# Chunks 1 to 3 of x by DMA transpose, and chunk 0's first layer with k as the outer loop, in a fused two-layer kernel

## The chip, the cores and the metric

One core of one Trainium2 chip. The metric is the device time of one execution in microseconds (us). "Span" is the time from the first to the last instruction in a profile; it is about 1.8 us shorter than the device time of the same run. A run is called slow when it is over 1.5% above the fastest run of its kernel.

Engines in the profile: PE is TensorE (PEld its weight loads), ACT is ScalarE, DVE is VectorE, POOL is GpSimd, SP issues DMA. A final q, as in SPq, means the engine's sequencer.

## The reference

```python
# x [1, 2048, 640], w1 [640, 1536], b1 [1536], w2 [1536, 640], b2 [640], all bfloat16
h = einsum("bsd,df->bsf", x, w1) + b1
h = relu(h) ** 2
out = einsum("bsf,fd->bsd", h, w2) + b2
```

## The kernel before

It works on four chunks of 512 rows of x. The contraction over D = 640 has five steps of 128, called k. F = 1536 gives twelve groups of 128, called j. For each chunk, PE makes twelve first-layer groups of five 128x512 matmuls, ACT adds b1 and applies relu, DVE squares, and PE then makes eight second-layer groups of twelve matmuls, 128x320 each (the very last group is cut in two). The first-layer matmuls of this kernel read x with D on the partitions (`rhs=xT[:, k, ...]`), so x is transposed. Here PE does that through PSUM, against an identity matrix, and DVE copies the result out. The transposes of chunk c+1 stand between the first-layer groups of chunk c.

```python
# loads on SP, in this order: x tiles 0-1, x tiles 2-3, then
sp.dma_start(out=w1_sb[:, :, 0:W1A], in_=w1_v[:, :, 0:W1A]).then_inc(s_w1a, 16)   # W1A = 384
sp.dma_start(out=w1_sb[:, :, W1A:F], in_=w1_v[:, :, W1A:F]).then_inc(s_w1b, 16)
# x chunk 1, b2, w2; POOL loads x chunks 2 and 3 after w2
# ... (cut)
def t_group(t):                    # one 128x640 tile of x: five PE transposes
    # ... waits (cut)
    for k in range(KD):
        ins = pe.transpose(out=t_ps[:, bank, k * P:(k + 1) * P],
                           in_=x_sb[:, t, k * P:(k + 1) * P], identity=ident[:])
def mm1_group(c, j):               # k is the inner loop
    # ... waits on s_w1a, s_w1b, s_xT (cut)
    for k in range(KD):
        ins = pe.matmul(h_ps[:, bank, :], lhsT=w1_sb[:, k, j * P:(j + 1) * P],
                        rhs=xT[:, k, c * CH:(c + 1) * CH],
                        start=(k == 0), stop=(k == KD - 1))
# ... (cut)
dummy(NDUM0)                       # 4 matmuls on zeros
# transpose of b1 (cut)
for t in range(TPC):
    t_group(t)                     # chunk 0
dummy(NDUM1)                       # 1 matmul on zeros
for c in range(NCH):
    for j in range(KF):
        mm1_group(c, j)
        if c + 1 < NCH and j in TPOS:          # TPOS = [6, 7, 8, 9]
            t_group((c + 1) * TPC + TPOS.index(j))
    # second layer of chunk c (cut)
# DVE: four copies of chunk 0's xT, then dve.wait_ge(s_b2, 16), then all squares
```

Of the kernel before, what the change touches and what calls it, by code (L numbers as in the profile page):

```python
# [5 lines left out]
ACT = mybir.ActivationFunctionType  # L6
ALU = mybir.AluOpType
BF16 = mybir.dt.bfloat16
FP32 = mybir.dt.float32


def bass_standalone__dense_activation_squared_relu__prompt_kernel(
# [8 lines left out]
    P = 128  # L21
# [10 lines left out]
    NH = 3  # L32
    NO = 3
    NT = 2
    NR = 4

    W1A = 384
    NDUM0 = 4
    NDUM1 = 1
    LAST_SPLIT = [(0, 320), (320, 160), (480, 160)]  # L40

    TPOS = [6, 7, 8, 9]

    x_v = x[0].rearrange("(i p) d -> p i d", p=P)
# [6 lines left out]
    with ExitStack() as es:  # L51
# [9 lines left out]
        x_sb = sb("x_sb", [P, NST, D], BF16)  # L61
# [12 lines left out]
        h_ps = ps("h_ps", [P, NH, 512], FP32)  # L74
        o_ps = ps("o_ps", [P, NO, 512], FP32)
        t_ps = ps("t_ps", [P, NT, 1024], BF16)
# [5 lines left out]
        s_xc1 = sem("s_xc1")  # L82
        s_xc2 = sem("s_xc2")
        s_xc3 = sem("s_xc3")
        s_w1a = sem("s_w1a")
        s_w1b = sem("s_w1b")
        s_w2 = sem("s_w2")
        s_b1 = sem("s_b1")
        s_b2 = sem("s_b2")
        s_b1ps = sem("s_b1ps")  # L90
# [11 lines left out]
        s_x0t = [s_xa, s_xa, s_xb, s_xb]  # L102
        s_xc = [None, s_xc1, s_xc2, s_xc3]
# [9 lines left out]
        NG = len(groups)  # L113
        out_dmas = []
# [6 lines left out]
        @block.sync  # L121
        def _(sp):
            sp.dma_start(out=x_sb[:, 0:2, :], in_=x_v[:, 0:2, :]).then_inc(s_xa, 16)  # L123
            sp.dma_start(out=x_sb[:, 2:4, :], in_=x_v[:, 2:4, :]).then_inc(s_xb, 16)  # L124
            sp.dma_start(out=w1_sb[:, :, 0:W1A], in_=w1_v[:, :, 0:W1A]).then_inc(s_w1a, 16)
            sp.dma_start(out=w1_sb[:, :, W1A:F], in_=w1_v[:, :, W1A:F]).then_inc(s_w1b, 16)
            sp.dma_start(out=x_sb[:, TPC:2 * TPC, :], in_=x_v[:, TPC:2 * TPC, :]).then_inc(s_xc1, 16)
            sp.dma_start(out=b2_bc[:], in_=b2_v).then_inc(s_b2, 16)
            sp.dma_start(out=w2_sb[:], in_=w2_v).then_inc(s_w2, 16)
            for (cnt, i, c0, nc_) in out_dmas:  # L130
                sp.wait_ge(s_osb, cnt)
                sp.dma_start(out=out_v[:, i, c0:c0 + nc_], in_=o_sb[:, i, c0:c0 + nc_]).then_inc(s_out, 16)
            sp.wait_ge(s_out, 16 * len(out_dmas))

        @block.gpsimd
        def _(pool):
            pool.memset(ident[:], 0.0).then_inc(s_ms, 1)  # L137
            pool.affine_select(  # L138
                out=ident[:],
                in_=ident[:],  # L140
                compare_op=ALU.not_equal,
                fill=1.0,
                base=0,
                pattern=[[-1, P]],
                channel_multiplier=1,
            ).wait_op(s_ms, 1, "sem-ge").then_inc(s_id, 1)
            pool.wait_ge(s_w2, 16)
            pool.dma_start(out=x_sb[:, 2 * TPC:3 * TPC, :], in_=x_v[:, 2 * TPC:3 * TPC, :]).then_inc(s_xc2, 16)  # L148
            pool.dma_start(out=x_sb[:, 3 * TPC:4 * TPC, :], in_=x_v[:, 3 * TPC:4 * TPC, :]).then_inc(s_xc3, 16)  # L149

        @block.tensor
        def _(pe):
            o_ps_bf = o_ps[:].bitcast(BF16)

            def dummy(nd):
                for _ in range(nd):
                    pe.matmul(o_ps[:, 0, :], lhsT=zeros[:, 0:P], rhs=zeros[:, :], start=True, stop=True)  # L157

            def t_group(t):
                c, i = divmod(t, TPC)  # L160
                bank = t % NT
                if c == 0:
                    if i % 2 == 0:
                        pe.wait_ge(s_x0t[i], 16)
                elif i == 0:
                    pe.wait_ge(s_xc[c], 16)
                for k in range(KD):
                    ins = pe.transpose(  # L168
                        out=t_ps[:, bank, k * P:(k + 1) * P],
                        in_=x_sb[:, t, k * P:(k + 1) * P],  # L170
                        identity=ident[:],
                    )
                    if k == 0 and t >= NT:
                        ins.wait_op(s_xT, t - NT + 1, "sem-ge")
                    if k == KD - 1:
                        ins.then_inc(s_T, 1)

            def mm1_group(c, j):
                n = c * KF + j
                bank = n % NH  # L180
                if c == 0 and j == 0:
                    pe.wait_ge(s_w1a, 16)
                if c == 0 and j * P == W1A:
                    pe.wait_ge(s_w1b, 16)
                if j == 0:
                    pe.wait_ge(s_xT, TPC * (c + 1))
                for k in range(KD):
                    ins = pe.matmul(  # L188
                        h_ps[:, bank, :],
                        lhsT=w1_sb[:, k, j * P:(j + 1) * P],  # L190
                        rhs=xT[:, k, c * CH:(c + 1) * CH],
                        start=(k == 0),
                        stop=(k == KD - 1),
                    )
                    if k == 0 and n >= NH:
                        ins.wait_op(s_r, n - NH + 1, "sem-ge")
                    if k == KD - 1:
                        ins.then_inc(s_h, 1)

            def mm2_group(m):  # L200
                i, c0, nc_ = groups[m]
                bank = m % NO
                c = i // TPC
                first_of_chunk = (i % TPC == 0) and c0 == 0
                if m == 0:
                    pe.wait_ge(s_w2, 16)
                if m == NO - 1:
                    pe.wait_ge(s_b1T, 1)
                if m >= NO and first_of_chunk:
                    pe.wait_ge(s_osb, m - NO + 1)  # L210
                for j in range(KF):
                    ins = pe.matmul(  # L212
                        o_ps[:, bank, 0:nc_],
# [4 lines left out]
                    )  # L218
                    if first_of_chunk:
                        ins.wait_op(s_r2, c * KF + j + 1, "sem-ge")  # L220
                    elif j == 0 and m >= NO:
                        ins.wait_op(s_osb, m - NO + 1, "sem-ge")
                    if j == KF - 1:
                        ins.then_inc(s_o, 1)

            pe.wait_ge(s_z, 1)
            dummy(NDUM0)
            pe.wait_ge(s_id, 1)
            pe.wait_ge(s_b1, 16)
            pe.transpose(  # L230
                out=o_ps_bf[:, NO - 1, 0:KF],
                in_=b1_row[:, :],
                identity=ident[0:KF, 0:KF],
            ).then_inc(s_b1ps, 1)
            for t in range(TPC):
                t_group(t)
            dummy(NDUM1)

            m = 0
            for c in range(NCH):  # L240
                for j in range(KF):
                    mm1_group(c, j)
                    if c + 1 < NCH and j in TPOS:
                        t_group((c + 1) * TPC + TPOS.index(j))
# [5 lines left out]
        def _(act):  # L250
            o_ps_bf = o_ps[:].bitcast(BF16)
            act.dma_start(out=b1_row[:], in_=b1_v).then_inc(s_b1, 16)
            act.activation(out=junk[:, 0:1], in_=zeros[:, 0:1], func=ACT.Relu).wait_op(s_z, 1, "sem-ge")  # L253
            act.activation(out=b1T[:], in_=o_ps_bf[:, NO - 1, 0:KF], func=ACT.Identity).wait_op(  # L254
                s_b1ps, 1, "sem-ge"
            ).then_inc(s_b1T, 1)
            act.wait_ge(s_b1T, 1)
            for n in range(NCH * KF):
                c, j = divmod(n, KF)
                if n >= NR:  # L260
                    act.wait_ge(s_r2, n - NR + 1)
                act.activation(  # L262
                    out=r_sb[:, n % NR, :],
                    in_=h_ps[:, n % NH, :],
# [3 lines left out]
                ).wait_op(s_h, n + 1, "sem-ge").then_inc(s_r, 1)  # L268

        @block.vector  # L270
        def _(dve):
            def t_evac(t):
                bank = t % NT
                dve.tensor_copy(  # L274
                    out=xT[:, :, t * P:(t + 1) * P],
                    in_=t_ps[:, bank, 0:KD * P].rearrange("p (k s) -> p k s", k=KD),
                ).wait_op(s_T, t + 1, "sem-ge").then_inc(s_xT, 1)

            def square(c, j):
                n = c * KF + j  # L280
                dve.tensor_tensor(  # L281
# [4 lines left out]
                ).wait_op(s_r, n + 1, "sem-ge").then_inc(s_r2, 1)  # L286

            def o_evac(m):
                i, c0, nc_ = groups[m]
                dve.tensor_tensor(  # L290
                    out=o_sb[:, i, c0:c0 + nc_],
                    in0=o_ps[:, m % NO, 0:nc_],
                    in1=b2_bc[:, c0:c0 + nc_],
                    op=ALU.add,
                ).wait_op(s_o, m + 1, "sem-ge").then_inc(s_osb, 1)

            dve.memset(zeros[:], 0.0).then_inc(s_z, 1)  # L297
            for t in range(TPC):
                t_evac(t)
            dve.wait_ge(s_b2, 16)  # L300
            m = 0
            for c in range(NCH):
                for j in range(KF):
                    if c + 1 < NCH and j in TPOS:
                        t_evac((c + 1) * TPC + TPOS.index(j))
                    square(c, j)
# [31 lines left out]
```

## Time and profile before

| | before |
|---|---|
| device time, median of the first 4 runs | 120.69 us (120.03 to 122.18) |
| span of the first profile (a slow run, 122.18 us) | 120.4 us |
| PE busy | 114.2 us, 95% of the span |
| first matmul on w1 | 8.50 us |

The first view is the chain that ended last, in order of time, merged: start, duration, what ran. It is followed back from the last instruction to whatever released each step.

```profile
1.74 6.71 DMA w_sb<-in_w_dram
8.45 0.05 issue
8.50 7.24 PE h_ps L188 x23
...
18.33 0.28 PE t_ps L168 x5
18.61 1.08 PE h_ps L188 x5
...
24.84 13.04 PE o_ps L212 x96
...
51.95 13.04 PE o_ps L212 x96
...
92.15 10.74 PE h_ps L188 x49
...
105.05 13.08 PE o_ps L212 x108
```

From 8.50 us, when the first part of w1 has landed, to the end, the chain lies on PE. Steady rates can be read from it: 0.216 us per first-layer matmul (1.08 for five), 0.136 per second-layer matmul (13.04 for 96), and 0.28 us for five transposes. The line of 7.24 us for 23 matmuls does not fit the first rate: 0.31 us each.

The timeline of this kernel from 6 to 12.8 us shows why (start, duration, engine, line, operation; in brackets the idle time before it):

```profile
6.30 0.63 PE L157 MATMUL o_ps<-zeros 128*128 128x512 bf16 x1
8.49 0.13 PEld L188 LDWEIGHTS h_ps<-xT,w_sb 128*128 128x128 bf16 x2 [2.15 <-DMA w_sb<-in_w_dram]
8.50 4.65 PE L188 MATMUL h_ps<-xT,w_sb 128*128 128x512 bf16 x11 [1.56 <-DMA w_sb<-in_w_dram]
8.90 0.15 PEld L188 LDWEIGHTS h_ps<-xT,w_sb 128*128 128x128 bf16 x1 [0.28 <-issue]
9.33 0.15 PEld L188 LDWEIGHTS h_ps<-xT,w_sb 128*128 128x128 bf16 x1 [0.28 <-issue]
...
12.31 0.15 PEld L188 LDWEIGHTS h_ps<-xT,w_sb 128*128 128x128 bf16 x1 [0.28 <-issue]
```

Weight loads start 0.43 us apart and take 0.15 us where later ones take 0.10. PE runs at half its later rate for the first ten matmuls or so, which costs about 2.1 us (10 x 0.21). What ends the stretch, and what sets its length, this trace does not show. The profile prints a granted clock of 1.00 for the whole run, but that says nothing here: the trace holds no clock record before 12.80 us, which is just where the slow stretch ends, and time without a record is printed as 1.00. So it is the spacing of the instructions that shows the slow stretch.

### The profile page before, as it was taken

Reading aid. Unit: us, or ns where it says so; the run is one execution under the profiler, and the core shown is the slowest. Engines: PE = TensorE matmul, PEld = TensorE weight load, DVE = VectorE, ACT = ScalarE, POOL = GpSimd, SP = SyncE. Lnnn points to the kernel's source line nnn. Section 1 sums busy time; section 2 is a strip of 40 time slices with the busy share of each in tenths; the row PEclk is TensorE's granted clock in tenths of the full one; section 3 lists DMA queues with packets and bytes.
Section 4 is the critical chain, followed back from the end, with each engine's and each line's share of the span. In section 5 each row is a group of like instructions: output and inputs, shape, how many; then the busy total and the mean of one; then the engine's idle time right before and its main releaser. Section 6 shows DMA issues by size and latency. Waiting matters only on the chain.

```text
span 120.4 us, 1706 instructions
## 1 busy us (share of the span) xinstructions
PE 114.2 (95%) x714; PEld 67.9 (56%) x722; DVE 43.6 (36%) x98; ACT 34.7 (29%) x51; POOL 2.3 (2%) x8
## 2 busy tenths in 40 slices
PE   6749999999999999999999999999999999999992
PEld 1513445567776445567776445567776444477781
DVE  0330067542233337542233337542233334433331
ACT  4002464530000664530000664530000666610000
POOL 2000002300000000000000000000000000000000
PEclk9999999999999999999999999999999999999999
DMA  3999991671101100001101100001101100001112
GB/s 92 271 334 392 321 353 39 177 259 54 37 26 51 54 0 0 0 3 54 42 26 46 54 3 0 5 0 54 35 26 48 54 5 0 0 0 54 54 54 54
DMA packets 6991, 9.44 MB, mean 78 GB/s; under 512 B 712, under 2 KB 6088, under 8 KB 6984
## 3 DMA queue, kind: packets, MB, share of 16 engines
q1 hardware_dynamic: 6672, 8.03, 19.9%
q0 software_dynamic: 288, 1.31, 3.4%
q8 instruction: 5, 0.08, 0.3%
q14 instruction: 2, 0.02, 0.1%
q10 hardware_dynamic: 24, 0.00, 0.0%
HBM read 6.72 MB, written 2.62 MB: 78 GB/s over the span
## 4 chain that ended last, share of the span: by engine, by line
PE 91%; DMA 6%; SPq 1%; issue 1%; DVE 0%
PE h_ps L188 45%; PE o_ps L212 43%; DMA w_sb<-in_w_dram 6%; PE t_ps L168 3%; SPq L124 0%; SPq L123 0%; DVE o_sb L290 0%
## 5 line engine op out<-in xcount | busy, mean ns | idle before, releaser
L188 PE MATMUL h_ps<-xT,w_sb 128*128 128x512 bf16 x232 | 55.3, 390 | 2.0 <-DMA w_sb<-in_w_dram 1.6
L262 ACT ACTIVATE r_sb<-h_ps,b1T 128x512 bf16<-128x512 f32 x48 | 33.0, 687 | 69.2 <-PE h_ps L188 68.8
L212 PE MATMUL o_ps<-w_sb,r2T 128*128 128x320 bf16 (+1 forms) x396 | 52.8, 295 | 0.0
L212 PEld LDWEIGHTS o_ps<-w_sb,r2T 128*128 128x128 bf16 x396 | 38.1, 98 | 14.9
L188 PEld LDWEIGHTS h_ps<-xT,w_sb 128*128 128x128 bf16 x240 | 23.4, 100 | 28.5 <-issue 2.8
L281 DVE TENSOR_TENSOR r2T<-r_sb 128x512 bf16<-128x512 bf16 x48 | 20.2, 425 | 31.5 <-ACT r_sb L262 23.5
L290 DVE TENSOR_TENSOR o_sb<-o_ps,b_bc 128x320 bf16<-128x320 f32 (+1 forms) x33 | 15.9, 482 | 33.5 <-PE o_ps L212 33.5
L274 DVE COPY xT<-t_ps 128x640 bf16<-128x640 bf16 x16 | 7.9, 492 | 9.0 <-PE t_ps L168 8.9
L168 PEld LDWEIGHTS t_ps<-ident,x_sb 128*128 128x128 bf16 x80 | 6.2, 108 | 4.0 <-DMA x_sb<-in_x_dram 0.7
L168 PE MATMUL t_ps<-ident,x_sb 128*128 128x128 bf16 x80 | 7.8, 242 | 0.7 <-DMA x_sb<-in_x_dram 0.6
L157 PE MATMUL o_ps<-zeros 128*128 128x512 bf16 x5 | 2.5, 629 | 1.2 <-DVE zeros L297 1.2
L253 ACT ACT_TABLE_LOAD x1 | 1.3, 1283 | 1.4 <-PEq L323 1.4
L157 PEld LDWEIGHTS o_ps<-zeros 128*128 128x128 bf16 x5 | 0.6, 136 | 1.7 <-DVE zeros L297 1.2
L148 POOL DMA_DIRECT2D x_sb<-in_x_dram x1 | 0.9, 885 | 19.1 <-DMA w_sb<-in_w_dram 19.1
L149 POOL DMA_DIRECT2D x_sb<-in_x_dram x1 | 0.8, 751 | 0.0
L230 PEld LDWEIGHTS o_ps<-ident,b_row 12*128 12x128 bf16 x1 | 0.1, 98 | 1.0 <-issue 1.0
L297 DVE MEMSET zeros<- 128x256 uint32 x1 | 0.3, 272 | 0.9 <-PEq L323 0.9
L254 ACT ACTIVATE b1T<-o_ps 128x12 f32<-128x12 bf16 x1 | 0.2, 181 | 0.4 <-PE o_ps L230 0.4
L138 POOL TENSOR_SCALAR_AFFINE_SELECT ident<-ident 128x128 bf16<-128x128 bf16 x1 | 0.3, 289 | 0.1
L230 PE MATMUL o_ps<-ident,b_row 12*128 12x12 bf16 x1 | 0.2, 162 | 0.1
L137 POOL MEMSET ident<- 128x128 bf16 x1 | 0.2, 205 | 0.3 <-POOLq L323 0.3
L253 ACT ACTIVATE junk<-zeros 128x1 f32<-128x1 bf16 x1 | 0.2, 203 | 0.0
(4 smaller groups left out, 0.4 us busy)
## 6 DMA issues: line engine op xcount, KB each, us to landing
out_dram<-o_sb SPq DMA_DIRECT2D x15, 160.0 KB, 1.8
w_sb<-in_w_dram SPq DMA_DIRECT2D x1, 1920.0 KB, 15.2
w_sb<-in_w_dram SPq DMA_DIRECT2D x1, 1440.0 KB, 9.9
x_sb<-in_x_dram POOLq DMA_DIRECT2D x2, 640.0 KB, 5.3
x_sb<-in_x_dram SPq DMA_DIRECT2D x2, 320.0 KB, 3.3
x_sb<-in_x_dram SPq DMA_DIRECT2D x1, 640.0 KB, 11.0
w_sb<-in_w_dram SPq DMA_DIRECT2D x1, 480.0 KB, 6.7
b_bc<-in_b_dram SPq DMA_DIRECT2D x1, 160.0 KB, 11.1
```

The costliest lines, as they stand in the source:

```text
L148: pool.dma_start(out=x_sb[:, 2 * TPC:3 * TPC, :], in_=x_v[:, 2 * TPC:3 * TPC, :]).then_inc(s_xc2, 16)
L149: pool.dma_start(out=x_sb[:, 3 * TPC:4 * TPC, :], in_=x_v[:, 3 * TPC:4 * TPC, :]).then_inc(s_xc3, 16)
L157: pe.matmul(o_ps[:, 0, :], lhsT=zeros[:, 0:P], rhs=zeros[:, :], start=True, stop=True)
L168: ins = pe.transpose(out=t_ps[:, bank, k * P:(k + 1) * P], in_=x_sb[:, t, k * P:(k + 1) * P], identity=ident[:],)
L188: ins = pe.matmul(h_ps[:, bank, :], lhsT=w1_sb[:, k, j * P:(j + 1) * P], rhs=xT[:, k, c * CH:(c + 1) * CH], start=(k == 0), stop=(k == KD ...
L212: ins = pe.matmul(o_ps[:, bank, 0:nc_], lhsT=r2T[:, j, i * P:(i + 1) * P], rhs=w2_sb[:, j, c0:c0 + nc_], start=(j == 0), stop=(j == KF - 1),)
L230: pe.transpose(out=o_ps_bf[:, NO - 1, 0:KF], in_=b1_row[:, :], identity=ident[0:KF, 0:KF],).then_inc(s_b1ps, 1)
L253: act.activation(out=junk[:, 0:1], in_=zeros[:, 0:1], func=ACT.Relu).wait_op(s_z, 1, "sem-ge")
L262: act.activation(out=r_sb[:, n % NR, :], in_=h_ps[:, n % NH, :], func=ACT.Relu, bias=b1T[:, j:j + 1], scale=1.0,).wait_op(s_h, n + 1, "sem ...
L274: dve.tensor_copy(out=xT[:, :, t * P:(t + 1) * P], in_=t_ps[:, bank, 0:KD * P].rearrange("p (k s) -> p k s", k=KD),).wait_op(s_T, t + 1, " ...
L281: dve.tensor_tensor(out=r2T[:, j, c * CH:(c + 1) * CH], in0=r_sb[:, n % NR, :], in1=r_sb[:, n % NR, :], op=ALU.mult,).wait_op(s_r, n + 1, ...
L290: dve.tensor_tensor(out=o_sb[:, i, c0:c0 + nc_], in0=o_ps[:, m % NO, 0:nc_], in1=b2_bc[:, c0:c0 + nc_], op=ALU.add,).wait_op(s_o, m + 1, " ...
```

## The change

The intent is twofold. The PE transposes of chunks 1 to 3 are to leave the critical engine, with the transposing done by the DMA on the way in. And chunk 0 is to start as soon as one k slice of w1 has landed: with k outside, eight groups can each use slice 0 while slice 1 is under way. The eight groups of the pass hold a PSUM bank each, so the pass borrows the second layer's and the transposes' banks.

```diff
-            sp.dma_start(out=w1_sb[:, :, 0:W1A], in_=w1_v[:, :, 0:W1A]).then_inc(s_w1a, 16)
-            sp.dma_start(out=w1_sb[:, :, W1A:F], in_=w1_v[:, :, W1A:F]).then_inc(s_w1b, 16)
-            sp.dma_start(out=x_sb[:, TPC:2 * TPC, :], in_=x_v[:, TPC:2 * TPC, :]).then_inc(s_xc1, 16)
+            for k in range(KD):
+                sp.dma_start(out=w1_sb[:, k, :], in_=w1_v[:, k, :]).then_inc(s_w1k[k], 16)
 ... (b2, w2; then, after all loads have landed:)
+            for c in range(1, NCH + 1):
+                if c < NCH:
+                    sp.dma_start_transpose(
+                        out=xT[:, :, c * CH:(c + 1) * CH], in_=x2[c * CH:(c + 1) * CH, :]
+                    ).then_inc(s_xTc[c], 16)
+                    spw.wait_all([(s_xTc[c], 16)])
+                # ... the stores of chunk c-1, and a wait until they have landed (cut)
 ... (PE)
-            dummy(NDUM1)                # and NDUM0 = 4 becomes 5
+            for k in range(KD):
+                for j in range(NPASS):   # NPASS = 8
+                    # ... waits: slice k; xT of chunk 0 (cut)
+                    mm1_matmul(j, k, extra)
+            for j in range(NPASS, KF):
+                for k in range(KD):
+                    mm1_matmul(j, k, [(s_w1k[k], 16)])
 ... (later chunks: mm1 with k inside, waiting on s_xTc[c]; no t_group among them)
```

Four smaller things come along. A helper emits waits only where they are still needed. The wait of DVE on b2 moves from before the squares to the output additions. The last transposed tile of chunk 0 is copied out in two parts. And b1 is loaded through SP, before the w1 slices, and no longer through ACT.

## The prediction

Its fourth step is about the DMA transposes that bring in chunks 1 to 3, 640 KB each.

> **What bounds the kernel now.** TensorE, from 8.5 us on. In the chain of waits PE has 91% of the span: first-layer matmuls 45%, second-layer 43%, transposes 3%; before them stand 6.7 us of w1 load. Read in order of time, PE is released by the first w1 slice at 8.50 and then has no gap over 0.05 us until 118.1. Steady rates from the same view: 1.08 us per five 128x512 matmuls, 13.04 us per second-layer chunk of 96, 0.28 us per five transposes. The first ten or so matmuls start 0.43 us apart, later ones 0.216: about 2.1 us of slow start.
>
> **What changes.**
> 1. Sixty PE transposes (12 groups at 0.28 us) leave the critical chain: -3.3 us. Cross-check in the chain: the first layer takes 14.0 us in chunks 1 and 2 and 12.9 in chunk 3, which has no transposes among its matmuls.
> 2. PE starts earlier. It now waits for x and the 480 KB w1 slice, in 768-byte rows, landing at 8.45. After, the first slice is 384 KB in 3 KB rows. I expect the first real matmul near 7.2 us (6.8 to 8.0): -1.3 us. A later slice lands about each 1.1 us (384 KB at the roughly 370 GB/s of the load stage), while a pass of eight takes 3.4 us slow and 1.7 fast, so no pass waits.
> 3. New stall in chunk 0. K-outer over eight banks finishes no group until the fifth pass, so ACT begins all twelve activations (687 ns each) there. From the pass's start, ACT needs 0.4 + 12 x 0.70 = 8.8 us, the last square 0.48 more: 9.3. PE reaches the last matmul of the first output group after 1.73 + 4.3 + 1.5 = 7.5. Cost: +1.8 us, all critical.
> 4. [...] The first is issued when all loads have landed (about 18 us, earlier than w2's 20 now as one x load is gone), and is needed near 37 us: 19 us of room. The others follow the previous chunk's stores (about 39 and 65) and have about 24 us. [...] No trace here has such a transfer yet. I take 4 to 12 us, hidden.
>
> **Sum.** -3.3 - 1.3 + 1.8 = -2.8 us: 117.5 us, range 115.8 to 120.5. Faster by over 2%: 0.60; within 2%: 0.27; slower: 0.13.
>
> **What would show it.** (1) No transposes among the chain's first-layer pieces after chunk 0; chunks 1 and 2 at 12.95 us like chunk 3. (2) First 128x512 matmul on w1 near 7.2 us. (3) Waits of output matmuls on the squares in chunk 0, 1.5 to 2 us together, ACT back to back for 8.3 us there. (4) DMA transposes landing well within 19 us of issue, and no first-layer wait on xT in chunks 1 to 3.
>
> **What would make it wrong.** DMA transposes above 19 us (slower by 5 us or more, with PE perhaps returning to the slow rate after each gap). A slow-start stretch of other length: the new idle pattern could shift it by 2 us either way. A straggling DMA that delays the first w1 slice would eat step 2.

## The result

| | before | after |
|---|---|---|
| device time, median | 120.54 us (16 runs) | 115.97 us (11 runs) |
| lowest to highest | 119.46 to 122.42 | 115.20 to 118.96 |
| ratio of fast runs | | 0.9641, 95% interval 0.9600 to 0.9683 |
| span of the first profile | 120.4 (slow run) | 113.6 (fast run) |

A ratio is the mean time of one kernel's fast runs over that of the other's of the same rounds, so it is not quite the ratio of the medians. The change makes the kernel 3.6% faster.

The chain of the changed kernel, in order of time:

```profile
6.65 0.05 issue
6.70 0.81 PE h_ps L243 x3
7.50 0.65 PE o_ps L243 x3
8.15 0.43 PE t_ps L243 x2
...
13.76 0.23 PE h_ps L243
13.99 0.02 issue
14.02 1.85 ACT r_sb L323 x3
...
21.10 0.44 DVE r2T L348
21.53 0.05 issue
21.58 11.72 PE o_ps L262 x85
33.30 0.05 issue
33.35 10.74 PE h_ps L243 x49
...
98.23 13.09 PE o_ps L262 x108
```

Three readings. The first matmul on w1 starts at 6.70 us and the matmuls follow each other every 0.216 us from the very first (0.65 for three): there is no slow stretch in this profile. (That is not a property of the change: a variant below with the same start has one.) From 14.02 to 21.58 the chain leaves PE for ACT and DVE, which is the new stall that the prediction spoke of. And no transposes stand between the first-layer groups of the later chunks.

The SP queue's DMA transposes, in the list of DMA issues (out<-in, operation, count, median us from issue to landing):

```profile
xT<-in_x_dram SPq DMA_TRANSPOSE x3, 5.1
```

In the trace they land at 23.2, 40.7 and 66.8 us. Their chunks are first read at 33.3, 59.3 and 85.3, so there are 10 us or more of slack.

### The profile page after: what moved, and what is told of

The parts are those of the page before. It is cut to its first block, busy times and chain, and to the rows that moved or that the text cites. A ratio compares the mean times of both kernels' runs of the same rounds, so it can differ in the third digit from the quotient of the medians.

```text
span 113.6 us, 1583 instructions
## 1 busy us (share of the span) xinstructions
PE 108.5 (96%) x655; PEld 63.6 (56%) x662; DVE 38.5 (34%) x87; ACT 33.5 (29%) x51; POOL 0.7 (1%) x6
## 4 chain that ended last, share of the span: by engine, by line
PE 86%; issue 4%; ACT 3%; DMA 3%; DVE 2%
PE o_ps L262 45%; PE h_ps L243 37%; ACT r_sb L323 3%; DMA x_sb<-in_x_dram 3%; PE o_ps L243 2%; PE t_ps L243 1%; DVE xT L341 1%; PE t_ps L229 1%; DVE r2T L348 1%; DVE o_sb L357 0%
## 5 line engine op out<-in xcount | busy, mean ns | idle before, releaser
L243 PE MATMUL h_ps<-xT,w_sb 128*128 128x512 bf16 x204 | 46.0, 379 | 0.9 <-DVE xT L341 0.5
L323 ACT ACTIVATE r_sb<-h_ps,b1T 128x512 bf16<-128x512 f32 x42 | 28.5, 691 | 61.7 <-PE h_ps L243 61.7
L243 PEld LDWEIGHTS h_ps<-xT,w_sb 128*128 128x128 bf16 x210 | 20.5, 98 | 24.7 <-DVE xT L341 0.7
L243 PE MATMUL o_ps<-xT,w_sb 128*128 128x512 bf16 x20 | 5.3, 379 | 0.0
L243 PEld LDWEIGHTS o_ps<-xT,w_sb 128*128 128x128 bf16 x20 | 1.9, 97 | 2.4
L341 DVE COPY xT<-t_ps 128x640 bf16<-128x640 bf16 (+1 forms) x4 | 1.9, 474 | 3.6 <-PE t_ps L229 3.5
L243 PE MATMUL t_ps<-xT,w_sb 128*128 128x512 bf16 x9 | 2.8, 379 | 0.0
L323 ACT ACTIVATE r_sb<-o_ps,b1T 128x512 bf16<-128x512 f32 x4 | 2.6, 719 | 0.0
L229 PE MATMUL t_ps<-ident,x_sb 128*128 128x128 bf16 x19 | 2.1, 268 | 0.4 <-DMA x_sb<-in_x_dram 0.4
L229 PEld LDWEIGHTS t_ps<-ident,x_sb 128*128 128x128 bf16 x19 | 1.5, 121 | 1.3 <-DMA x_sb<-in_x_dram 1.3
```

The lines of the kernel that those rows point to most:

```text
L229: ins = pw.emit(reqs if k == 0 else [], lambda: pe.transpose(out=dst, in_=x_sb[:, t, k * P:(k + 1) * P], identity=ident[:],))
L243: ins = pw.emit(reqs, lambda: pe.matmul(banks[bname], lhsT=w1_sb[:, k, j * P:(j + 1) * P], rhs=xT[:, k, c * CH:(c + 1) * CH], start=(k == ...
L323: aw.emit(reqs, lambda: act.activation(out=r_sb[:, n % NR, :], in_=banks[g1_bank[n]], func=ACT.Relu, bias=b1T[:, j:j + 1], scale=1.0,)).th ...
L341: dw.emit([(s_T, cnt)], lambda: dve.tensor_copy(out=xT[:, k0:k1, t * P:(t + 1) * P], in_=src.rearrange("p (k s) -> p k s", k=k1 - k0),)).t ...
```

## The experiments

Where a count of slow matmuls is given, it was counted in the trace as weight loads of real w1 data that took over 140 ns.

### The kernel before, again

No edit. The first profile of before was a slow run, so a fast one was needed to compare.

> The unchanged kernel before, to see how much of the 6.8 us between the first two profiles (120.4 and 113.6 us of span) is a slow run of the kernel before. Theory M (the matmul rate at the start varies): the stretch in which 128x512 matmuls start 0.43 us apart has another length in this profile (0 to 20 of them) whenever the span differs by more than 0.5 us, and everything from chunk 1 on takes the same time within 0.2 us. Rival D (a DMA landing late makes the spread): the first 128x512 matmul on w1 starts at another time than 8.5 us by as much as the spans differ. Ratio 1.00 +- 0.005.

Measured: ratio 1.0007 (0.9942 to 1.0073). The profiled run was a fast one, with a span of 118.5 us. Two slow matmuls on w1 against nine in the slow profile; first matmul at 7.32 us against 8.50; everything from chunk 1 on within 0.1 us (80.2 us in both). So both theories hold a part: of 1.9 us between the two spans, 1.2 us is the later landing of w1 and the rest lies in chunk 0.

The earlier start runs into other waits, in the chain of this run:

```profile
3.37 11.83 DMA b_bc<-in_b_dram
...
15.30 0.44 DVE r2T L281
...
15.82 0.70 ACT r_sb L262
...
16.56 1.25 PE h_ps L188 x5
```

DVE may not square before b2 has landed (15.2 us). ACT runs out of its four buffers, PE runs out of banks and idles 0.33 us. PE also waits 0.3 us for the second part of w1 at 11.5 us. In the kernel before, starting early was partly spent on such waits. The change takes both away, and the prediction saw neither, because in the slow profile PE came too late to meet them.

The fast pair gives the account of the change (us, read from the chains and timelines; "chunk 0" runs from the first w1 matmul to the end of its second layer):

| profiled run | first w1 matmul | chunk 0 | chunks 1 to 3 | span |
|---|---|---|---|---|
| before, fast | 7.32 | 28.69 | 80.2 | 118.5 |
| after, fast | 6.70 | 26.60 | 78.0 | 113.6 |
| difference | -0.6 | -2.1 | -2.2 | -4.9 |

Chunks 1 to 3 lose the eight transpose groups among their own first layers (8 x 0.28 = 2.2). Chunk 0 loses four (1.1) and gets a stall of about 0.5. The remaining 1.5 us is what the waits and the two slow matmuls had cost; it is found by difference, and its parts were not measured one by one.

### The DMA transposes alone

```diff
 (from before)
-            pool.wait_ge(s_w2, 16)
-            pool.dma_start(out=x_sb[:, 2 * TPC:3 * TPC, :], ...)   # and chunks 1 and 3
+                    sp.dma_start_transpose(
+                        out=xT[:, :, c * CH:(c + 1) * CH], in_=x[0][c * CH:(c + 1) * CH, :]
+                    ).then_inc(s_xc[c], 16)                          # placed as in the changed kernel
-                    if c + 1 < NCH and j in TPOS:
-                        t_group((c + 1) * TPC + TPOS.index(j))
```

> The kernel before with one half of the change: chunks 1 to 3 of x come by DMA transpose, PE and VectorE transposes of them are gone; chunk 0 stays as it was. If the critical chain loses just the 60 PE transposes: -3.3 us, ratio 0.972 (0.968 to 0.977), first w1 matmul still near 8.5 us, first-layer work of chunks 1 and 2 12.95 us. Rival: the DMA transposes cost something on the chain (late landing, a store delayed behind the transpose): ratio above 0.98.

Measured: ratio 0.9703 (0.9641 to 0.9766). The chain of this run:

```profile
12.35 9.87 PE h_ps L197 x45
22.22 13.04 PE o_ps L221 x96
35.26 12.95 PE h_ps L197 x60
48.21 13.04 PE o_ps L221 x96
61.25 12.95 PE h_ps L197 x60
```

Every first layer after chunk 0 is one piece of 12.95 us. The first w1 matmul was at 8.62 us. This half gives 3.0%, or 3.6 us of 120.1 (the mean of the fast runs of before in these rounds), close to the 12 x 0.28 = 3.4 us of removed transposes. The interval reaches from 2.3% to 3.6%, so a further gain from b2 landing earlier (13.4 us against 15.0 and 15.2 in the profiles of before, since one x load is gone) can be neither seen nor excluded.

None of its w1 matmuls is slow, although PE's work up to the first of them is that of the kernel before, whose two profiles have nine and two slow ones. The clock record of this trace begins at 6.85 us, before the first w1 matmul; that of the slow profile of before begins at 12.80, after its slow stretch. So the slow stretch comes and goes between executions that start alike.

### K-outer alone

This has six groups in the pass, so that the transposes of chunk 1 keep their two banks. It is made from the changed kernel, so the four smaller things listed above are in this half too, and it is not the loop order by itself.

```diff
 (from after)
-    NPASS = 8
+    NPASS = 6
-                    sp.dma_start_transpose(...)      # plain loads of x, PE transposes and
+                    # DVE copies at j in TPOS, as in the kernel before
```

> The other half: w1 by five k slices and chunk 0 k-outer (six banks in the pass instead of eight, so that the two transpose banks stay free), with PE transposes for chunks 1 to 3 as before. Theory S (earlier start and full matmul rate from the start): first w1 matmul near 6.7 us, 0.216 us apart at once, -1.8 us of start and 0 to -2 us of slow rate: ratio 0.970 to 0.985. Rival (the DMA transposes brought all of the gain and the reorder only moves a wait): ratio 0.993 or more.

Measured: ratio 0.989 (0.9814 to 0.9965). The profile fell in a slow run: start at 7.78 us, five matmuls at the full rate, then eight slow ones. Here the granted clock does show it (one digit for each 3 us, in tenths of full speed):

```profile
PEclk9995999999999999999999999999999999999999
```

The trace records half clock from 8.54 to 11.95 us, for 3.41 us. So "full rate at once" was a miss in this run, and the gain of 1.1% was below the 1.5 to 3% expected. The reorder gives something, but less than the transposes. How much cannot be told better than 0.3 to 1.9% from these rounds.

### Both, with six groups in the pass

```diff
 (from after)
-    NPASS = 8
+    NPASS = 6
```

> The changed kernel with six groups in the k-outer pass instead of eight. The stall of 0.6 us before the first output group should vanish, since ACT begins 1.7 us earlier: 0.3 to 0.7 us faster than the changed kernel, ratio to before 0.955 to 0.962; waits of output matmuls on squares under 0.1 us. Rival (shorter passes outrun the w1 slices): a wait on w1 of up to 0.5 us appears instead and the ratio stays at 0.964. If the two halves simply add, the ratio is the product of the two halves' ratios within 0.004.

Measured: ratio 0.9594 (0.9546 to 0.9642). The halves' ratios multiply to 0.9703 x 0.989 = 0.9596, so they add as far as these rounds can tell; their intervals (0.5 to 0.75% to each side) could hide an interaction of about 1 us. The chain of this run has no ACT or DVE step left before the first output group:

```profile
13.97 3.24 PE h_ps L243 x15
17.20 1.08 PE o_ps L243 x5
18.28 2.16 PE h_ps L243 x10
20.44 13.04 PE o_ps L262 x96
33.48 12.95 PE h_ps L243 x60
```

Chunk 0 takes 33.48 - 7.33 = 26.15 us, against 26.60 in the changed kernel. The stall therefore costs 0.45 us. Run once more beside the last version below, it gave:

> The six-group kernel again, on the same chip as the version meant to beat it. Ratio 0.956 to 0.963; no stall before the first output group (under 0.1 us, against 0.6 in the changed kernel); first w1 matmul between 6.7 and 7.4 us.

Ratio 0.9542 (0.947 to 0.9615), chunk 0 again 26.15 us, start at 7.20.

### The changed kernel, again

> The changed kernel once more, beside its variants on one chip: ratio 0.960 to 0.968. Its stall before the first output group (0.58 us in the first profile) comes again, 0.4 to 0.7 us, because it follows from eight activations released at once.

Ratio 0.9648 (0.9579 to 0.9717); start at 6.78 us, no slow matmul, chunk 0 again 26.60 us. The stall is a property of the kernel, not of a run. Its cause shows in the ACT timeline of the first profile of the changed kernel:

```profile
14.02 1.84 ACT L323 ACTIVATE r_sb<-h_ps,b1T 128x512 bf16<-128x512 f32 x3 [8.56 <-PE h_ps L243]
15.74 1.85 ACT L323 ACTIVATE r_sb<-o_ps,b1T 128x512 bf16<-128x512 f32 x3
17.45 1.30 ACT L323 ACTIVATE r_sb<-t_ps,b1T 128x512 bf16<-128x512 f32 x2
18.59 1.90 ACT L323 ACTIVATE r_sb<-h_ps,b1T 128x512 bf16<-128x512 f32 x3
20.30 0.76 ACT L323 ACTIVATE r_sb<-o_ps,b1T 128x512 bf16<-128x512 f32 x1
```

ACT idles until 14.02 and then works without a gap to 21.06. But twelve activations start only (20.30 - 14.02) / 11 = 0.57 us apart, though each is recorded as about 0.7 us long: they overlap. The prediction had put them 0.70 apart. The fast profile of the kernel before shows the same where ACT has a backlog: three activations of 0.69 us each take 1.84 us, so they start 0.58 us apart.

```profile
15.82 1.84 ACT L262 ACTIVATE r_sb<-h_ps,b1T 128x512 bf16<-128x512 f32 x3 [2.38 <-DVE r2T L281]
```

### The w1 slices without the reorder

```diff
 (from after)
-            for k in range(KD):
-                for j in range(NPASS):
+            for j in range(NPASS):
+                for k in range(KD):
```

> The changed kernel with its w1 slices, its eight banks and its DMA transposes, but the loops of the chunk 0 pass exchanged: group by group, all five k of one before the next. If the order is what lets PE use the early slices: group 0 has to wait for slice after slice (they land about 1.0 us apart, the fifth near 11 us), so PE has done only 5 matmuls of about 21 possible by 11 us: about 3.4 us lost at the start, the stall of 0.5 us before the output groups gone, so +2.5 to +3.2 us against the changed kernel, ratio to before 0.982 to 0.992. Rival (only the earlier arrival of small slices matters, or the landing of the slices is no limit): ratio within 0.005 of 0.964.

Measured: ratio 0.9929 (0.9853 to 1.0005), median 120.16 us. Against the changed kernel's ratio of 0.9641 that is 2.9% or about 3.5 us, give or take 1 us: far from the rival's forecast, and a little above the 2.5 to 3.2 expected. PE's rows of the timeline:

```profile
7.67 0.38 PE L243 MATMUL h_ps<-xT,w_sb 128*128 128x512 bf16 x1 [1.33 <-DMA w_sb<-in_w_dram]
8.87 0.38 PE L243 MATMUL h_ps<-xT,w_sb 128*128 128x512 bf16 x1 [0.82 <-DMA w_sb<-in_w_dram]
9.71 0.61 PE L243 MATMUL h_ps<-xT,w_sb 128*128 128x512 bf16 x1 [0.47 <-DMA w_sb<-in_w_dram]
10.62 0.61 PE L243 MATMUL h_ps<-xT,w_sb 128*128 128x512 bf16 x1 [0.30 <-DMA w_sb<-in_w_dram]
11.55 1.04 PE L243 MATMUL h_ps<-xT,w_sb 128*128 128x512 bf16 x2 [0.32 <-DMA w_sb<-in_w_dram]
```

Each matmul waits for its slice, as expected. What was not expected: PE falls back to half rate while it waits. The first two matmuls are recorded at 0.38 us, the next at 0.61; the granted clock is 0.58 from 9 to 12 us, 0.50 from 12 to 15 and 0.79 from 15 to 18 (in the trace's record, half clock from 9.46 to 16.29 us); ten weight loads are slow. The order of the loops is thus what makes the slices usable. That it also holds PE at its full rate is not shown: the k-outer profile above had eight slow matmuls as well.

### More matmuls on zeros before the first real one

```diff
 (from before)
-    NDUM1 = 1
+    NDUM1 = 5
```

> The kernel before with five instead of one 128x512 matmul on zeros between the transposes of chunk 0 and the first matmul on w1, so that PE has no long gap there. Theory W (the full matmul rate is granted after some microseconds of dense PE work, so gaps before the first w1 matmul put the slow stretch into real work): slow matmuls fall on the zeros, the real ones start 0.216 us apart; the spread of the times shrinks (highest minus lowest under 2 us, against 2.8 in the kernel before) and the fast runs are 0 to 1 us faster, ratio 0.990 to 1.000. Rival (the slow stretch begins with the real matmuls, whatever runs before): spread and ratio unchanged, slow matmuls again among the real ones.

Measured: ratio 0.9967 (0.99 to 1.0034), not told from 1. But all six runs were fast, with spans of 118.2 to 118.7 us, while the kernel before had 6 slow runs of 11 in the same rounds and spans of 117.7 to 120.6. In the profile all slow matmuls fall on zeros; none is left on w1:

```profile
6.73 0.15 PEld L157 LDWEIGHTS o_ps<-zeros 128*128 128x128 bf16 x1 [0.28 <-issue]
7.07 0.31 PEld L157 LDWEIGHTS o_ps<-zeros 128*128 128x128 bf16 x2 [0.19 <-issue]
8.17 1.04 PE L188 MATMUL h_ps<-xT,w_sb 128*128 128x512 bf16 x4 [0.30 <-DMA w_sb<-in_w_dram]
```

By device time the picture is less clean. "Slow" is counted from each kernel's own fastest run; by the line of the kernel before (121.25 us), two of these six, at 121.28 and 121.38, would be slow. Their spans are not longer than the others': the time from span to device time is 2.6 and 2.9 us in them, for a reason that the record does not show. The median of all runs fell from 121.78 to 120.46. This supports the theory that dense work before the first real matmul moves the slow stretch out of the real work, and that this stretch makes a good part of the spread. It rests on the six spans: the one profile proves little, since the kernel with the DMA transposes alone had no slow w1 matmul either, with a single matmul on zeros there.

### No matmuls on zeros

```diff
 (from after)
-    NDUM0 = 5
+    NDUM0 = 0
```

> The changed kernel without its five matmuls on zeros at the start. Theory W (full rate only after some microseconds of dense PE work): 8 to 16 of the first matmuls on w1 start 0.43 us apart in the profile, fast runs 0.5 to 2 us slower than the changed kernel's, ratio 0.970 to 0.982. Rival (the matmuls on zeros do nothing for the real ones, the phase is chance alone): ratio as the changed kernel's, 0.960 to 0.968.

Measured: ratio 0.9726 (0.9657 to 0.9794), median 117.01. The profile starts at 6.79 us like the changed kernel's (6.78 in the same rounds), then has five slow matmuls, fewer than the eight expected, and a span of 114.7 against 113.7: 1.0 us, as five times 0.21 says. The five matmuls on zeros, in a time when PE has nothing else to do, are worth about 1 us in this profile. The ratios of the same rounds (0.9726 against 0.9648) say the same, but their intervals overlap. The clock record fits: it begins at 9.01 us here, where the slow matmuls end, and at 5.02 in the first profile of the changed kernel, before its first w1 matmul (6.70).

### Every DMA transpose twice

```diff
 (from after)
                     spw.wait_all([(s_xTc[c], 16)])
+                    sp.dma_start_transpose(
+                        out=xT2[:, :, :], in_=x2[c * CH:(c + 1) * CH, :]
+                    ).then_inc(s_xT2, 16)
+                    spw.wait_all([(s_xT2, 16 * c)])
```

> The changed kernel with every DMA transpose issued a second time, into a spare tile that nobody reads, after the first has landed and before the stores. If the DMA transposes are hidden (landing 5 us after issue, 10 us or more before their chunk is read): ratio as the changed kernel's, 0.960 to 0.968, no first-layer wait on xT. Rival (they cost time somewhere, by the stores queued behind them or by their 256-byte packets): 1 us or more slower, ratio above 0.972.

Measured in the three timed runs: 115.74, 116.65 and 117.12 us, ratio 0.9628 (0.9539 to 0.9718). Doubling the transposes costs nothing that can be seen, so they are hidden, as far as three runs tell: a cost under about 1 us would not show.

The profiled execution of this kernel was an oddity: 407.68 us, with a correct result. PE ran every matmul at about a quarter of its rate for the whole run (60 first-layer matmuls in 49.15 us, 0.82 each), while the DMA transposes landed 4.7 to 5.3 us after issue as always. It is left out of every comparison, and its cause is open.

### A version meant to beat both

The six-group kernel with more matmuls on zeros (six before, three after the transposes) came first:

```diff
 (from after)
-    NPASS = 8
-    NDUM0 = 5
+    NPASS = 6
+    NDUM0 = 6
+    NDUM1 = 3            # dummy(NDUM1) after the transposes of chunk 0
```

> The six-group pass, with one more matmul on zeros before the transposes and three after them (PE idle there from about 6.0 to 7.3 us). Theory W: full rate from the first w1 matmul in nearly every run, so fewer slow runs and a median at or below that of the six-group kernel: ratio 0.953 to 0.962. Rival: the matmuls on zeros run into the landing of the first w1 slice and delay it by up to 0.4 us: ratio 0.960 to 0.965.

Measured: ratio 0.9553 (0.9478 to 0.9628), four fast runs of four, first w1 matmul at 7.17 us. It cannot be told from the six-group kernel by time. In its profile PE waits for the second slice (landed at 8.70 us) after the first pass of six, and its next matmul starts 0.37 us late (8.84, against 7.17 + 6 x 0.216 = 8.47): a pass of six lasts 1.3 us, and one slice came later than that. This is the rival that the six-group kernel was run against; its own two profiles show no such wait. Then the slices of the pass were cut to the columns that the pass reads, so that the first one is half as large:

```diff
 (from the last one)
-                sp.dma_start(out=w1_sb[:, k, :], in_=w1_v[:, k, :]).then_inc(s_w1k[k], 16)
+                sp.dma_start(out=w1_sb[:, k, 0:WH], in_=w1_v[:, k, 0:WH]).then_inc(s_w1k[k], 16)
+            sp.dma_start(out=w1_sb[:, :, WH:F], in_=w1_v[:, :, WH:F]).then_inc(s_w1r, 16)   # WH = 768
-    NDUM1 = 3
+    NDUM1 = 2
```

> A version meant to beat both (its first build failed on a slip): six-group pass; the w1 slices of the pass cut to its own 768 columns (192 KB each, the other columns follow in one transfer); one more matmul on zeros before and two after the transposes. If the landing of the first slice bounds the start (6.7 to 7.3 us in the six-group kernels), it now starts when the last transposed tile is copied, 6.5 to 6.8 us; no stall before the output groups: ratio 0.951 to 0.960, span below 113.4 us. Rival (what delays the landing is not the size of the slice): start at 7 us or later and ratio 0.956 to 0.962.

Measured: ratio 0.9529 (0.9469 to 0.959), median 114.93 us. All six runs were fast and lay between 114.83 and 115.14; the six-group kernel beside it lay between 114.65 and 117.54, with two slow runs. The first w1 matmul was at 6.59 us and chunk 0 took 26.15 us. The start lies where it was expected, but not for the expected reason: the last tile was copied by 6.34 us, and PE still waited for the slice, which landed at 6.46. The full slice landed at 6.56 to 6.65 us in three profiles of the eight-group kernels, so this one start does not show that the smaller slice is what made it early. It has the lowest median of all. Against the six-group kernel's fast runs (0.9542) the difference is inside the intervals, so what is shown is mainly that the spread went in these six runs.

## Why the prediction was right, and where its sum was off

The prediction said 117.5 us, 2.8 us of gain; measured were 115.97 us, and 3.6% of the fast mean of before (about 120.2) is 4.3 us. The mechanism was right, and one term of the sum was too large.

- **Step 1, the sixty transposes, -3.3 us.** Right. Chunks 1 and 2 fell to 12.95 us. The transposes alone gave 3.0%.
- **Step 2, the earlier start, -1.3 us, near 7.2 us (6.8 to 8.0).** Roughly right as a mean, wrong as one number. With the slices, eight profiles start at 6.70, 6.78, 6.79, 7.17, 7.20, 7.33, 7.67 and 7.78 (mean 7.18); with the two-part w1, four start at 7.32, 8.17, 8.50 and 8.62 (mean 8.15). The mean gain is 1.0 us. The prediction took its start from one slow run. It said that no pass would wait, which held for the eight-group pass; a pass of six waited once, for 0.37 us.
- **Step 3, the stall, +1.8 us.** This is the mis-sized term: it measured +0.45 us (26.60 against 26.15 us for chunk 0). The twelve activations were put 0.70 us apart, from their mean duration of 687 ns; they follow each other every 0.57. The slow profile that the prediction was made from does not show this, because PE feeds ACT too slowly there (starts 1.08 us apart or more). The fast profile of before, taken afterwards, does, as shown above. With its 0.58 us in place of 0.70 the stall comes out at about 0.4 us (1.8 less twelve times 0.12), an estimate from that profile.
- **Step 4, the DMA transposes hidden, 4 to 12 us each.** The range was the author's estimate; no trace before the change held such a transfer. Right: 5.1 us, 10 us or more of slack, and doubling them costs nothing that could be seen.
- **What was not in the sum.** The kernel before also lost time in its fast runs to the second part of w1 (0.3 us), to b2 in front of the squares (0.33 us of PE idle in one fast profile) and to the slow stretch. The prediction named the slow stretch as a risk "by 2 us either way", and kept it equal on both sides. The wait on b2 was not tried by itself, so its share stays an observation of one trace.

The stall's error of 1.35 us alone takes the forecast gain from 2.8 to about 4.2 us, close to the measured 4.3. This is partly luck, since a smaller gain at the start was offset by the waits that were not counted.

## What to carry to other kernels

A recorded duration is not the distance between two starts (0.69 us against 0.57 to 0.58 for ACT here): before you multiply it by a count, find a place in the trace where that engine runs back to back. Moving layout work from the critical engine to a transfer with 10 us of slack paid in full here (3.6 us gained, give or take 0.8, for 3.4 us of transposes), and doubling the hidden work is a cheap test that it is hidden. At the start of a kernel, order the loops so that each arriving slice feeds many outputs (about 3.5 us here), keep the pass short enough that the engine behind it can drain the banks (0.45 us between eight groups and six), and fill idle TensorE time with matmuls on zeros, which was worth about 1.0 us in one pair of profiles and here seems to narrow the spread too (spans of 118.2 to 118.7 us against 117.7 to 120.6). Where the rate of PE is in question, look at the spacing of its instructions: a printed clock of 1.00 can mean that there is no record, as before 12.80 us in the slow profile of the kernel before.

## What else the traces show

- The count of slow matmuls on w1 lay between zero and ten in profiles of the same kernel family, which is up to about 2.1 us or 1.8% of the span. Filling the gap with matmuls on zeros turned 6 slow runs of 11 into none of 6, each kernel counted from its own fastest run.
- The execution of 405.9 us ran at about a quarter of the usual rate throughout, with 0.82 us per 128x512 matmul against 0.216. Its trace holds no clock record at all, which the profile prints as 1.00; so a printed 1.00 does not show a full clock. In the run that waited for slices the half clock is recorded, for 6.83 us.
- Twenty 128x128 blocks in one DMA transpose landed 5.1 us after issue, 0.26 us each. That is 640 KB in 5.1 us, or 128 GB/s from issue to landing, and 2.7 to 3.1 us of it is time that SP is busy issuing.
- Back-to-back activations start 0.57 us apart and are recorded as 0.68 to 0.76 us long in the changed kernel, so they overlap by 0.11 to 0.19 us.
- The sixteen landing records of one transfer lie apart. In the changed kernel, the first of those of the first w1 slice is at 5.33 us and the last at 6.56; in the slow profile of the kernel before the spread was 2.7 us (5.78 to 8.45). PE starts after the last one: 0.05 us after it in that slow profile, and 0.13 to 0.14 us after it in seven profiles with slices, in which it landed at 6.46 to 7.65 us.
